# Attention with top-k, two MoE layers on one core: another order for epsilon, reciprocals, loads and the parts of a pair

## Chip, core and metric

The kernel runs on one core of one Trainium2 chip. The metric is the device time of one launch in microseconds (us); lower is better. Five engines take part, each with its own queue worked off in order: TensorE (PE), VectorE (DVE), ScalarE (ACT), GpSimd (POOL) and SyncE (SP), which here only issues DMAs.

## What is computed

Three layers follow one another on 4 batches of 576 tokens. Cut to what matters:

```python
scores = scale * np.matmul(q, k.transpose(0, 1, 3, 2))      # 4 batches, 8 heads, 576 x 64
kth = np.partition(scores, -32, axis=-1)[..., -32:-31]      # keep the 32 largest of a row
scores = np.where(scores >= kth, scores, -1e9)
attn = softmax(scores)
x = np.matmul(attn, v)                                      # -> 2304 x 512

h = x @ w_in                                                # MoE 1: 512 -> 2048 -> 512
x = (np.maximum(h, 0) + alpha * np.minimum(h, 0)) @ w_out

do = x @ w_skip > 0                                         # MoE 2: 8 experts, the best one per token
e = argmax(x[do] @ w_gate); p = its softmax weight
x[do] += p * (np.maximum(x[do] @ w1[e], 0) @ w2[e])
```

## The kernel before

Every product of 32-bit numbers is made of three matmuls on a rounded "high" part and the rest, the "low" part. ScalarE rounds the high part, and GpSimd makes the low part by a subtraction (helper `sub`, L109). So each operand of a matmul costs ScalarE one or two copies and GpSimd one subtraction.

Attention goes through 20 pairs of heads (4 pairs in each of 5 pieces of work: batch 0 in two pieces of 2 and 3 units, batches 1 to 3 in one piece of 5 units). A unit is 128 query rows of both heads; the last unit of a batch is a mixed one with the 64 left-over rows of both heads. There are 80 units, and one pass of the main loop (a step) works on several of them at once, at different stages. A step has 14 slots. The table `STEP` lists in which slot (first number) of the step of unit kx which stage is written, and for which unit (second number, relative to kx). After each slot the function `slot` adds deferred work (the list `late`, counted in slots) and a share of the MoE work (`todo`, `rowq`). The order so written is the order in each engine's queue; nothing is reordered later.

The stages of a unit: `scores` (PE, L390), `copy` (ACT takes the scores out of PSUM into sb, L395), `fold` (DVE, L411, six maxima and minima that sort the 576 scores roughly), four `round`s (DVE: MAX8 L420 finds eight maxima, MATCH_REPLACE8 L423 takes them out), `exp` (ACT, L443), `weights` (DVE, L449: masks the exponentials by the 32nd value and sums them), `eps` (ACT, L454: adds 1e-9 to the sum), `recip` (DVE, L458, and on ACT, L461, a copy of the reciprocals spread over 128 columns, tile rb), `turn` (PE transposes of the weights, L476 to L482), `evac` (ACT copies of them to PT, L488 to L499), `values` (PE, L506 and L510) and `out` (DVE multiplies by the reciprocal, L517; ACT and POOL make the two parts of x).

The parts of a pair (`heads`) prepare q and k for the next pair: `load` (six DMAs by SP into the tiles nat and nat_t, L315 and L316), `turn(0)` for q, `turn(1)` for k and `turn_t` for the 64 left-over rows. Each turn is a few PE transposes (L330, L336) into a PSUM tile pt, and `HL` = 3 slots later two ACT copies (L323, L324; for the left-over rows also L341, L344), followed by the POOL subtraction on 512 columns. The tile pt has two buffers, which the transposes of the weights use as well.

Two more things stand in the way of these stages. Before batch 0 is through, the 32 pieces of MoE 1's weights are converted (tile cv: ACT, DVE L278 and L279, POOL, and DMAs both ways). After each piece of work `rows` writes the routing for MoE 2: `logits` (PE L693, ACT copies lg, L700 and L702), `route` (DVE, from L737), and the ranks.

GpSimd's subtractions of MoE 1 (tile g) are held back by `between` in slots 9 to 13 and 0, until the fold is written; those of a pair's parts are not.

Of the kernel before, what the change touches and what calls it, by code (L numbers as in the profile page):

```python
# [8 lines left out]
F32R = mybir.dt.float32r  # L9
# [12 lines left out]
SPREAD = 1.0  # L22
NSLOT = 14
STEP = [(0, 2, "scores", 0), (0, 0, "exp", 0), (0, 0, "exp", 1), (0, 1, "fold"),
        (1, 2, "copy", 0), (1, -1, "eps"),
        (2, 1, "round", 0),
        (4, 2, "scores", 1), (4, -1, "turn", 0), (4, 1, "round", 1), (4, 2, "copy", 1),
        (5, -1, "recip"), (5, -1, "turn", 1),
        (6, -1, "evac", 0), (6, -2, "out"), (6, 1, "round", 2),
        (7, -1, "evac", 1),  # L30
        (8, 1, "round", 3), (8, 1, "rest"),
        (9, -1, "turn", 2),
        (10, 0, "heads"), (10, 0, "weights", 0), (10, -1, "evac", 2),
        (11, 0, "weights", 1),
        (13, -1, "values")]
AHEAD = 2
EC = 32
PH = 9
ECC = 1.9
CL = 2  # L40
DV = 8
# [18 lines left out]
def kernel(  # L60
# [241 lines left out]
    def heads(b, p, i):  # L302

        hd = dict(vb=vbd[i], qb=qbd[i])
        nats = {}

        def load():

            hd["q"] = att.tile([128, 2, SB], F32R, name="qT", tag="qT", bufs=2)
            hd["k"] = att.tile([128, 2, S + TL], F32R, name="kT", tag="kT", bufs=2)  # L310
            tail = att.tile([128, 2, D], F32, name="nat_t", tag="nat_t", bufs=2)
            for s, src in enumerate((q, k)):
                nat = att.tile([128, SF, 2, D], F32, name="nat", tag="nat", bufs=2)
                for h in range(2):
                    nc.sync.dma_start(nat[:, :, h, :], src[b, 2 * p + h, 0:SB, :].rearrange("(p r) d -> p r d", p=128))  # L315
                nc.sync.dma_start(tail[s * TL:(s + 1) * TL], src[b, 2 * p:2 * p + 2, SB:S, :].rearrange("h t d -> t h d"))  # L316
                nats[s] = nat
            nats[2] = tail

        def part(t, pt):  # L320

            raw = att.tile([128, 512], F32, name="raw_", tag="raw_", bufs=2)[:, 0:pt.shape[1]]
            nc.scalar.activation(t[:, 0], pt, AF.Copy)  # L323
            nc.scalar.activation(raw, pt, AF.Copy)  # L324
            sub(t[:, 1], raw, t[:, 0].bitcast(F32))

        def turn(s):
            pt = ptile()
            for r in range(SF):
                nc.tensor.transpose(pt[:, r * 128:(r + 1) * 128], nats[s][:, r].rearrange("p h d -> p (h d)"), ident)  # L330
            c0 = TL
            late.append((HL, lambda: part(hd["k"][:, :, c0:c0 + SB] if s else hd["q"], pt)))

        def turn_t():
            pt = ptile()
            nc.tensor.transpose(pt[:, 0:128], nats[2].rearrange("p h d -> p (h d)"), ident)  # L336

            def copies():

                raw = att.tile([128, 512], F32, name="raw_", tag="raw_", bufs=2)[:, 0:TL]  # L340
                nc.scalar.activation(raw, pt[:, 0:TL], AF.Copy)  # L341
                for h in range(2):
                    gp = slice(h * 64, (h + 1) * 64)
                    nc.scalar.activation(hd["qb"][gp, 0, gp], pt[gp, 0:TL], AF.Copy)  # L344
                    sub(hd["qb"][gp, 1, gp], raw[gp], hd["qb"][gp, 0, gp].bitcast(F32))
                part(hd["k"][:, :, 0:TL], pt[:, TL:128])
                nc.gpsimd.tensor_copy(hd["k"][:, :, S:S + TL], hd["k"][:, :, 0:TL].bitcast(F32))

            late.append((HL, copies))

        def loadv():
            vt = att.tile([128, 2, SF, D], F32, name="vt", tag="vt", bufs=2)
            hd["vt"] = vt
            nc.sync.dma_start(vt.rearrange("p h r d -> p h (r d)"),
                              v[b, 2 * p:2 * p + 2, 0:SB, :].rearrange("h (p r) d -> p h (r d)", p=128))
            for h in range(2):
                nc.sync.dma_start(vbd[i][h * 64:(h + 1) * 64, h * 64:(h + 1) * 64], v[b, 2 * p + h, SB:S, :])

        hd["v"] = loadv
        return hd, [load, lambda: turn(0), lambda: turn(1), turn_t]  # L360

    class Unit:

# [92 lines left out]
        def recip(self):  # L456
            st = self.st
            nc.vector.reciprocal(st[:, 2, self.n_], st[:, 1, self.n_])  # L458
            if not self.mix:
                self.rb = att.tile([128, 2, 64], F32, name="rb", tag="rb", bufs=2)  # L460
                nc.scalar.activation(self.rb, st[:, 2, :, None].to_broadcast([128, 2, 64]), AF.Copy)  # L461
# [218 lines left out]
    def rows(b, us, colof, x2t, hook, then):  # L680
# [121 lines left out]

            return [scatter] + none + [then]

        parts = [(lambda: not early[0] and rroom(), None), (0.1, logits), (0, None), (0.1, route)]
        for i in range(nu):
            parts += [(rroom, None), (0.45, lambda i=i: row(i)), (0, None)]
            if i == min(1, nu - 1):
# [266 lines left out]
    def main(work, exact, hooks=(lambda: [], lambda: [])):  # L1075
# [27 lines left out]
        last = {s_[0]: kx for kx, s_ in enumerate(steps)}  # L1103
        hds, hq, vq = {}, [], {}

        def push_heads(i):
            hd, parts = heads(*pairs[i], i % 2)
            hds[i] = hd
            hq.extend(parts)
            if i > 1:  # L1110

                vq[i] = hd["v"]
# [72 lines left out]
        for kx in range(-2, K + 2):  # L1185
# [19 lines left out]
            for x in range(NSLOT):  # L1205
# [3 lines left out]
                for at, d, name, *a in STEP:  # L1209
                    if at != x:  # L1210
                        continue
                    if name == "heads":
                        for f in hmine:
                            f()
                    elif d in U:
                        getattr(U[d], name)(*a)
# [204 lines left out]
```

## Time and profile before

| what | value |
|---|---|
| median of 3 runs | 1148.2 us (1145.6 to 1149.4) |
| profiled execution | 1146.64 us, its span 1144.8 us |
| busy: PE, DVE, ACT, POOL | 85%, 84%, 65%, 40% of the span |
| attention (first fold to last) | about 26 to 833 us |
| mean granted TensorE clock | 0.928 of full speed |

Busy shares are means over stages. From about 60 us to the end of attention DVE is busy nearly all the time; after it, the rest of MoE 1 and MoE 2 are carried by PE, then DVE and PE. PE's busy time is modelled, one matmul from its issue to its end, so that matmuls that follow closely count as overlapping; how close they can follow is read from trains of them.

### The profile page before, as it was taken

Reading aid. Unit: us, or ns where it says so; the run is one execution under the profiler, and the core shown is the slowest. Engines: PE = TensorE matmul, PEld = TensorE weight load, DVE = VectorE, ACT = ScalarE, POOL = GpSimd, SP = SyncE. Lnnn points to the kernel's source line nnn. Section 1 sums busy time; section 2 is a strip of 40 time slices with the busy share of each in tenths; the row PEclk is TensorE's granted clock in tenths of the full one; section 3 lists DMA queues with packets and bytes.
Section 4 is the critical chain, followed back from the end, with each engine's and each line's share of the span. In section 5 each row is a group of like instructions: output and inputs, shape, how many; then the busy total and the mean of one; then the engine's idle time right before and its main releaser. Section 6 shows DMA issues by size and latency. Waiting matters only on the chain.

```text
span 1144.8 us, 21810 instructions
## 1 busy us (share of the span) xinstructions
PE 976.2 (85%) x7214; PEld 855.7 (75%) x7214; DVE 957.6 (84%) x2906; ACT 738.7 (65%) x1970; POOL 453.9 (40%) x591
## 2 busy tenths in 40 slices
PE   1255657989898987898998999899999999898996
PEld 1143436879777875787997998789899999687884
DVE  5799999999999999999999889999933331799872
ACT  5576666866777665776677567767734452597761
POOL 5445543643334331244235344423435343228111
PEclk9996566999999995899999999999999999799998
DMA  8977764567544530224324253332337863699870
GB/s 233 336 220 229 216 184 124 188 191 232 187 136 154 179 130 21 69 75 142 97 84 142 75 171 93 105 122 75 112 111 274 298 221 111 195 372 385 316 276 15
DMA packets 129771, 197.37 MB, mean 172 GB/s; under 512 B 62766, under 2 KB 92462, under 8 KB 119408
## 3 DMA queue, kind: packets, MB, share of 16 engines
q1 hardware_dynamic: 115632, 107.48, 29.9%
q0 software_dynamic: 14016, 88.40, 22.6%
q8 instruction: 59, 0.97, 0.3%
q14 instruction: 64, 0.52, 0.2%
HBM read 167.44 MB, written 29.71 MB: 172 GB/s over the span
## 4 chain that ended last, share of the span: by engine, by line
PE 42%; DVE 42%; ACT 5%; issue 4%; DMA 4%; POOL 2%; SPq 1%; POOLq 0%; DVEq 0%; ACTq 0%
PE pm L627 14%; DVE v L420 8%; PE pm L578 8%; DVE F L411 6%; DVE Ex L449 6%; DVE F L423 5%; DVE m L411 5%; PE px L1003 4%; PE pm L985 3%; PE px L510 3%; PE pt L476 3%; PE ps L390 3%; DVE rn L595 3%; DMA nat<-in_q_dram 2%; DVE cv L278 2%
## 5 line engine op out<-in xcount | busy, mean ns | idle before, releaser
L627 PE MATMUL pm<-g,wr 128*128 128x288 f32 (+2 forms) x1536 | 237.3, 303 | 7.2 <-POOL g L109 7.2
L578 PE MATMUL pm<-x,wr 128*128 128x288 f32 (+2 forms) x1536 | 238.9, 304 | 4.0 <-ACT x L519 2.9
L627 PEld LDWEIGHTS pm<-g,wr 128*128 128x128 f32 x1536 | 209.0, 189 | 15.1 <-POOL g L109 8.8
L578 PEld LDWEIGHTS pm<-x,wr 128*128 128x128 f32 x1536 | 211.2, 191 | 10.4 <-issue 5.3
L420 DVE MAX8 v<-F 128x8 f32<-128x72 f32 (+2 forms) x576 | 214.0, 406 | 1.0
L395 ACT ACTIVATE sb<-ps 128x288 f32<-128x288 f32 x288 | 104.9, 411 | 89.3 <-PE ps L390 70.3
L109 POOL TENSOR_TENSOR g<-rn,g 128x288 fp32r<-128x288 f32 (+2 forms) x128 | 108.2, 853 | 123.2 <-ACT g L609 52.5
L390 PE MATMUL ps<-kT,qT 64*128 64x288 f32 x768 | 106.4, 363 | 38.6 <-ACT sb L395 15.7
L449 DVE SCALAR_TENSOR_TENSOR Ex<-sb,v,Ex 128x576 f32<-128x576 f32 x144 | 124.5, 891 | 0.0
L423 DVE MATCH_REPLACE8 F<-v,F 128x72 f32<-128x72 f32 (+1 forms) x432 | 122.7, 289 | 0.0
L390 PEld LDWEIGHTS ps<-kT,qT 64*128 64x128 f32 x768 | 69.2, 210 | 68.2 <-ACT sb L395 19.8
L109 POOL TENSOR_TENSOR x<-xf,x 128x128 fp32r<-128x128 f32 (+1 forms) x80 | 38.7, 483 | 177.6 <-ACT x L519 164.6
L443 ACT ACTIVATE Ex<-sb,st 128x576 f32<-128x576 f32 x144 | 105.0, 780 | 0.0
L595 DVE SCALAR_TENSOR_TENSOR rn<-rn,nalpha 128x288 f32<-128x288 f32 (+2 forms) x128 | 72.5, 566 | 34.3 <-ACT rn L589 31.7
L476 PE MATMUL pt<-ident,Ex 128*128 128x128 f32 x576 | 92.6, 302 | 0.0
L510 PE MATMUL px<-PT,vt 128*64 128x128 f32 (+1 forms) x1280 | 92.0, 292 | 0.0
L488 ACT ACTIVATE PT<-pt 128x512 f32<-128x512 f32 x144 | 86.0, 598 | 2.3 <-PE pt L476 2.0
L588 ACT ACTIVATE rn<-pm 128x288 f32<-128x288 f32 (+2 forms) x128 | 52.7, 412 | 45.3 <-PE pm L578 44.6
L476 PEld LDWEIGHTS pt<-ident,Ex 128*128 128x128 f32 x576 | 72.2, 154 | 11.1 <-issue 6.5
L510 PEld LDWEIGHTS px<-PT,vt 128*64 128x64 f32 x1280 | 72.5, 150 | 10.2 <-issue 2.9
L411 DVE TENSOR_TENSOR F<-m 128x144 f32<-128x144 f32 (+2 forms) x240 | 78.2, 377 | 0.0
L609 ACT ACTIVATE g<-rn 128x288 fp32r<-128x288 f32 (+2 forms) x128 | 56.4, 448 | 23.0 <-DVE rn L595 22.9
(367 smaller groups left out, 1839.2 us busy)
## 6 DMA issues: line engine op xcount, KB each, us to landing
wraw<-in_moe_w_dram SPq DMA_DIRECT2D x88, 512.0 KB, 6.0
wr<-win POOLq DMA_DIRECT2D x40, 1024.0 KB, 5.2
wr<-wout POOLq DMA_DIRECT2D x40, 1024.0 KB, 5.2
cv<-in_moe_w_in_dram SPq DMA_DIRECT2D x16, 512.0 KB, 5.3
win<-cv SPq DMA_DIRECT2D x16, 512.0 KB, 5.4
cv<-in_moe_w_out_dram SPq DMA_DIRECT2D x16, 512.0 KB, 4.1
wout<-cv SPq DMA_DIRECT2D x32, 256.0 KB, 4.5
vt<-in_v_dram SPq DMA_DIRECT2D x20, 256.0 KB, 3.0
```

The lines of the kernel that those rows point to most:

```text
L109: i = nc.gpsimd.tensor_tensor(o, a, b, op=OP.subtract)
L390: nc.tensor.matmul(self.ps[h, j][:, 0:HALF], lhsT=hd["q"][gp, a, u * 128:(u + 1) * 128], rhs=hd["k"][gp, b_, c0:c0 + HALF], **se)
L411: gate[0] = nc.vector.tensor_tensor(o[:, n_], a[:, n_, 0:w], a[:, n_, w:2 * w], op=op)
L420: nc.vector.max(v8[:, h, r, :], F[:, h, 0:w])
L423: nc.vector.match_replace(out=F[:, h, 0:w], in_to_replace=v8[:, h, r, :], in_values=F[:, h, 0:w], imm_value=NEG)
L443: nc.scalar.activation(self.Ex[:, h, :], self.sb[:, h, :], AF.Exp, bias=self.st[:, 0, h:h + 1], scale=0.125)
L449: nc.vector.scalar_tensor_tensor(Ex[:, h, :], sb[:, h, :], v8[:, h, 3, 7:8], Ex[:, h, :], op0=OP.is_ge, op1=OP.mult, accum_out=st[:, 1, h: ...
L476: nc.tensor.transpose(pt[:, c * 128:(c + 1) * 128], P[:, c0:c0 + 128], ident)
L510: nc.tensor.matmul(x[h * 64:(h + 1) * 64, 0:n], lhsT=hd["vt"][:, h, c, :], rhs=rhs, start=False, stop=(c == SF - 1))
L578: nc.tensor.matmul(hp[:, 0:n], lhsT=w[:, (f % 2) * 8 + a * 4 + d, :], rhs=x[:, d, c0:c1], start=(i == 0), stop=(i == 3 * KD - 1))
L595: nc.vector.scalar_tensor_tensor(rn[:, 0, 0:n], rn[:, 1, 0:n], nalpha[:, f:f + 1], rn[:, 0, 0:n], op0=OP.mult, op1=OP.add)
L627: nc.tensor.matmul(op_[:, 0:n], lhsT=w[:, 2 * f + a, :], rhs=g[(hf + ch) * 8 + f, sg][:, gg, 0:n], start=(i == 0), stop=(i == ni - 1))
```

## The change

The table of slots and four functions change.

- `eps` moves from slot 1 of the next step to slot 13 of the unit's own step, behind `weights`.
- `recip` keeps the DVE instruction and moves from slot 5 to slot 2, right behind the fold. The spread of the reciprocals becomes a stage of its own, `spread`, in slot 7 behind the second `evac`.
- The parts of a pair written in a step are dealt alternately to slot 3 and slot 10 (before: all in slot 10). In a step with one part, it goes to slot 3.
- The load of a pair's q and k goes to the end of the list of parts of the pair before it, so it is issued a pair ahead; the very first list has both loads. The tiles qT and kT are taken in `turn(0)` instead of in `load`.
- `route` is written `RD` = 5 slots after `logits` instead of one.

```diff
@@ STEP
         (0, 0, "exp", 0), (0, 0, "exp", 1), (0, 1, "fold"),
-        (1, 2, "copy", 0), (1, -1, "eps"),
-        (2, 1, "round", 0),
+        (1, 2, "copy", 0),
+        (2, -1, "recip"), (2, 1, "round", 0),
+        (3, 0, "heads", 0),
         (4, 2, "scores", 1), (4, -1, "turn", 0), (4, 1, "round", 1), (4, 2, "copy", 1),
-        (5, -1, "recip"), (5, -1, "turn", 1),
+        (5, -1, "turn", 1),
         (6, -1, "evac", 0), (6, -2, "out"), (6, 1, "round", 2),
-        (7, -1, "evac", 1),
+        (7, -1, "evac", 1), (7, -1, "spread"),
         (8, 1, "round", 3), (8, 1, "rest"),
         (9, -1, "turn", 2),
-        (10, 0, "heads"), (10, 0, "weights", 0), (10, -1, "evac", 2),
+        (10, 0, "heads", 1), (10, 0, "weights", 0), (10, -1, "evac", 2),
         (11, 0, "weights", 1),
-        (13, -1, "values")]
+        (13, -1, "values"), (13, 0, "eps")]
+RD = 5
...
@@ heads
-        return hd, [load, lambda: turn(0), lambda: turn(1), turn_t]
+        hd["load"] = load
+        return hd, [lambda: turn(0), lambda: turn(1), turn_t]
...
@@ Unit
         def recip(self):
             st = self.st
             nc.vector.reciprocal(st[:, 2, self.n_], st[:, 1, self.n_])
+
+        def spread(self):
+            st = self.st
             if not self.mix:
                 self.rb = att.tile([128, 2, 64], F32, name="rb", tag="rb", bufs=2)
                 nc.scalar.activation(self.rb, st[:, 2, :, None].to_broadcast([128, 2, 64]), AF.Copy)
...
@@ rows
-        parts = [(lambda: not early[0] and rroom(), None), (0.1, logits), (0, None), (0.1, route)]
+        parts = [(lambda: not early[0] and rroom(), None), (0.1, logits)] + [(0, None)] * RD + [(0.1, route)]
...
@@ main
         def push_heads(i):
-            hd, parts = heads(*pairs[i], i % 2)
+            if not ahead:
+                ahead[i] = heads(*pairs[i], i % 2)
+                hq.append(ahead[i][0]["load"])
+            hd, parts = ahead.pop(i)
             hds[i] = hd
             hq.extend(parts)
+            if i + 1 < len(pairs):
+
+                ahead[i + 1] = heads(*pairs[i + 1], (i + 1) % 2)
+                hq.append(ahead[i + 1][0]["load"])
...
                     if name == "heads":
-                        for f in hmine:
+                        for f in hmine[a[0]::2]:
                             f()
```

How the queues change shows best in the instructions themselves. Line numbers behind the change are those of the changed file (L454 eps is L458 there, L461 is L468, L323 and L324 are L322 and L323).

First ScalarE, one step in batch 1 in which k of the next pair is prepared (kT and raw are the two copies of the part, Ex the exponentials, sb the scores, st the sums, rb the spread reciprocals, PT the transposed weights, x the result). Before:

```order
L323 ACTIVATE kT<-pt 128x512
L324 ACTIVATE raw__4652<-pt 128x512
L443 ACTIVATE Ex<-sb,st 128x576 x2
L395 ACTIVATE sb<-ps 128x288 x2
L454 ACTIVATE st<-st 128x2
L636 ACTIVATE x2t<-pm 128x320
L395 ACTIVATE sb<-ps 128x288 x2
L461 ACTIVATE rb<-st 128x128
L488 ACTIVATE PT<-pt 128x512
L519 ACTIVATE x<-xf 128x64
L488 ACTIVATE PT<-pt 128x512
```

With the change:

```order
L458 ACTIVATE st<-st 128x2
L447 ACTIVATE Ex<-sb,st 128x576
L399 ACTIVATE sb<-ps 128x288 x4
L643 ACTIVATE x2t<-pm 128x320
L322 ACTIVATE kT<-pt 128x512
L323 ACTIVATE raw__4508<-pt 128x512
L495 ACTIVATE PT<-pt 128x512
L526 ACTIVATE x<-xf 128x128
L495 ACTIVATE PT<-pt 128x512
L468 ACTIVATE rb<-st 128x128
```

The epsilon now stands ahead of the exponentials and the score copies, the part's two copies behind them, and the spread behind both copies of PT.

Then VectorE, one step (xf is the result times its reciprocal, m and F are the fold's). Before:

```order
L449 SCALAR_TENSOR_TENSOR Ex,st<-sb,v_4423,Ex 128x576 x2
L411 TENSOR_TENSOR m<-sb 128x2x288
L411 TENSOR_TENSOR F<-sb 128x2x288
L411 TENSOR_TENSOR m<-m 128x2x144
L411 TENSOR_TENSOR F<-m 128x2x144
L411 TENSOR_TENSOR F<-m 128x2x72 x2
L420 MAX v_4423<-F 128x8 x2
L423 MATCH_REPLACE F<-v_4423,F 128x72 x2
L420 MAX v_4423<-F 128x8 x2
L423 MATCH_REPLACE F<-v_4423,F 128x72 x2
L458 RECIPROCAL st<-st 128x2
L517 TENSOR_TENSOR xf<-px,R 128x64
```

With the change:

```order
L453 SCALAR_TENSOR_TENSOR Ex,st<-sb,v_4447,Ex 128x576 x2
L415 TENSOR_TENSOR m<-sb 128x2x288
L415 TENSOR_TENSOR F<-sb 128x2x288
L415 TENSOR_TENSOR m<-m 128x2x144
L415 TENSOR_TENSOR F<-m 128x2x144
L415 TENSOR_TENSOR F<-m 128x2x72 x2
L462 RECIPROCAL st<-st 128x2
L424 MAX v_4447<-F 128x8 x2
L427 MATCH_REPLACE F<-v_4447,F 128x72 x2
```

The reciprocal stands two rounds earlier, with only the fold between it and the sums.

Last SyncE at the start of the program (cv and win are the weights to convert and converted, vt and vbd are v). Before, behind the loads of the first pair:

```order
L316 DMA nat_t<-in_k_dram 64x2x64
L254 DMA cv<-in_moe_w_in_dram 128x4x256 x3
L291 DMA win_127<-cv 128x1024
L254 DMA cv<-in_moe_w_in_dram 128x4x256
L354 DMA vt<-in_v_dram 128x2x256
L357 DMA vbd_93<-in_v_dram 64x64 x2
L291 DMA win_127<-cv 128x1024
```

and only nine rows further the loads of the second pair. With the change:

```order
L315 DMA nat_t<-in_k_dram 64x2x64
L256 DMA cv<-in_moe_w_in_dram 128x4x256 x2
L314 DMA nat<-in_q_dram 128x4x64 x2
L315 DMA nat_t<-in_q_dram 64x2x64
L314 DMA nat<-in_k_dram 128x4x64 x2
L315 DMA nat_t<-in_k_dram 64x2x64
L256 DMA cv<-in_moe_w_in_dram 128x4x256
```

The second pair's six loads follow two weight loads behind the first pair's.

## Rows read from the trace of the kernel before

**Rows 1.** Stretch; busy us of PE, PEld, DVE, ACT, POOL; clock, DMA share, GB/s.

```profile
60.00:180.00 120.00, 68.78 (x352) 49.78 (x351) 119.31 (x297) 84.43 (x211) 57.41 (x52) 0.68 0.67 202
500.00:700.00 200.00, 190.64 (x1622) 172.94 (x1620) 187.41 (x657) 138.29 (x423) 81.88 (x116) 0.98 0.37 115
700.00:850.00 150.00, 145.20 (x1246) 132.59 (x1243) 137.53 (x474) 102.72 (x315) 56.13 (x81) 1.00 0.30 100
```

**Rows 2.** Waits of DVE between 60 and 837 us: total, times, longest.

```profile
DVE st L458 <- ACT st L454: 13.6, 10, 2.8
DVE rc L737 <- ACT lg L702: 3.9, 1, 3.9
```

**Rows 3.** Timeline of DVE, 374 to 383 us: start, duration, line, operation.

```profile
374.75 1.83 DVE L411 TENSOR_TENSOR F<-sb 128x576 f32<-128x576 f32 x1
...
382.19 0.80 DVE L449 SCALAR_TENSOR_TENSOR Ex<-sb,v,Ex 128x576 f32<-128x576 f32 x1
...
382.92 1.90 DVE L449 SCALAR_TENSOR_TENSOR Ex<-sb,v,Ex 128x576 f32<-128x576 f32 x1
```

**Rows 4.** Timeline of POOL at the same times.

```profile
374.27 1.70 POOL L109 TENSOR_TENSOR qT<-raw__4521,qT 128x512 fp32r<-128x512 f32 x1 [2.35 <-ACT raw__4521 L324]
...
382.92 1.29 POOL L109 TENSOR_TENSOR kT<-raw__4652,kT 128x512 fp32r<-128x512 f32 x1 [2.00 <-ACT raw__4652 L324]
```

**Rows 5.** DVE's operations by line and shape, 60 to 850 us: total, mean ns.

```profile
L449 DVE SCALAR_TENSOR_TENSOR Ex<-sb,v,Ex 128x576 f32<-128x576 f32 x142 | 122.9, 892 | 0.0
...
L411 DVE TENSOR_TENSOR m<-sb 128x576 f32<-128x576 f32 x62 | 53.9, 870 | 0.0
L411 DVE TENSOR_TENSOR F<-sb 128x576 f32<-128x576 f32 x62 | 53.8, 868 | 0.0
```

**Rows 6.** One line's durations in ns, least, median and most.

```profile
L411 DVE TENSOR_TENSOR m<-sb x80: 442/748/1843, 26.1 to 831.3; 128x576 f32<-128x576 f32 x64, 128x288 f32<-128x288 f32 x16
```

**Rows 7.** A MAX8 pair on DVE under a subtraction on POOL, timeline.

```profile
81.41 1.27 POOL L109 TENSOR_TENSOR cv<-cv 128x512 fp32r<-128x512 f32 x1 [2.45 <-ACT cv L285]
...
82.19 0.81 DVE L420 MAX8 v<-F 128x8 f32<-128x288 f32 x2
...
370.45 0.81 DVE L420 MAX8 v<-F 128x8 f32<-128x288 f32 x2
```

**Rows 8.** The second pair's q at the start: PE, ACT, DVE, timeline.

```profile
34.81 1.09 PE L330 MATMUL pt<-ident,nat 128*128 128x128 f32 x4 [14.05 <-DMA nat<-in_q_dram]
...
35.93 0.60 ACT L323 ACTIVATE qT<-pt 128x512 fp32r<-128x512 f32 x1 [10.39 <-PE pt L330]
...
38.15 0.77 DVE L278 SCALAR_TENSOR_TENSOR cv<-cv 128x512 int32<-128x512 int32 x1 [7.08 <-ACT cv L274]
```

**Rows 9.** PE's operations between 500 and 700 us by line.

```profile
L627 PE MATMUL pm<-g,wr 128*128 128x288 f32 x384 | 62.1, 306 | 4.6 <-POOL g L109 4.6
L578 PE MATMUL pm<-x,wr 128*128 128x288 f32 x372 | 59.1, 304 | 0.0
```

**Rows 10.** The chain that ended last: a train of 192 matmuls, start and length.

```profile
920.21 25.44 PE pm L578 x192
```

**Rows 11.** PE's timeline in the step from 384.75 us.

```profile
386.25 1.09 PE L476 MATMUL pt<-ident,Ex 128*128 128x128 f32 x8
387.10 2.00 PE L627 MATMUL pm<-g,wr 128*128 128x320 f32 x12
389.65 0.33 PE L478 MATMUL pt<-ident,Ex 128*128 128x128 f32 x1 [0.55 <-ACT PT L488]
```

**Rows 12.** ACT's timeline around the same step.

```profile
381.75 0.60 ACT L323 ACTIVATE kT<-pt 128x512 fp32r<-128x512 f32 x1
...
382.72 1.44 ACT L443 ACTIVATE Ex<-sb,st 128x576 f32<-128x576 f32 x2
...
384.92 0.71 ACT L395 ACTIVATE sb<-ps 128x288 f32<-128x288 f32 x2 [0.76 <-DVE Ex L449]
```

**Rows 13.** ACT's wait for the reciprocal, whole run: total, times, longest.

```profile
ACT rb L461 <- DVE st L458: 43.2, 29, 3.6
```

More of the change, by code (lines that the diff above doesn't have):

```diff
@@ L307, in load @@
         def load():
-            hd["q"] = att.tile([128, 2, SB], F32R, name="qT", tag="qT", bufs=2)
-            hd["k"] = att.tile([128, 2, S + TL], F32R, name="kT", tag="kT", bufs=2)
             tail = att.tile([128, 2, D], F32, name="nat_t", tag="nat_t", bufs=2)
@@ L327, in turn @@
         def turn(s):
+            if s == 0:
+                hd["q"] = att.tile([128, 2, SB], F32R, name="qT", tag="qT", bufs=2)
+                hd["k"] = att.tile([128, 2, S + TL], F32R, name="kT", tag="kT", bufs=2)
             pt = ptile()
@@ L1104, in main @@
         hds, hq, vq = {}, [], {}
+        ahead = {}
         def push_heads(i):
-            hd, parts = heads(*pairs[i], i % 2)
+            if not ahead:
+                ahead[i] = heads(*pairs[i], i % 2)
+                hq.append(ahead[i][0]["load"])
+            hd, parts = ahead.pop(i)
             hds[i] = hd
             hq.extend(parts)
+            if i + 1 < len(pairs):
+                ahead[i + 1] = heads(*pairs[i + 1], (i + 1) % 2)
+                hq.append(ahead[i + 1][0]["load"])
             if i > 1:
```

## Prediction

> **What bounds the kernel now.** I read the stretches first: which engine has no idle time left, and where. From 60 to 180 us DVE is busy 119.3 of 120 us, from 500 to 700 us 187.4 of 200 [rows 1]. So through attention nearly every microsecond of DVE's own time, and every wait of DVE, is a microsecond of the kernel. Next I read DVE's waits there: 13.6 us in ten waits of the reciprocal for the epsilon, 3.9 us of the routing for the logits [rows 2]. That is little; the rest must be in the lengths of DVE's instructions. So the third view is one shape's mean against its undisturbed length. The masking (L449) takes 0.80 us when nothing disturbs it [rows 3] and 892 ns in the mean of 142; the two widest operations of the fold (L411) have a median of 748 ns [rows 6] and means of 870 and 868 ns [rows 5]. The timeline says why: the fold's second operation takes 1.83 us and a masking 1.90 us [rows 3] exactly where GpSimd makes the low part of q and of k for the next pair [rows 4]. Both operations read two tiles. MAX8 does not mind: a pair of them takes 0.81 us under a subtraction of GpSimd and 0.81 us without one [rows 7].
>
> The other engine near its limit is PE. Its busy time of 190.6 of 200 us [rows 1] is modelled and says little, so I count. In a train of 192 nothing but MoE matmuls, one takes 25.44 / 192 = 0.1325 us [rows 10]. From 500 to 700 us there are 384 + 372 of them [rows 9], 100 us; the other 1622 - 756 = 866 instructions take at most (387.10 - 386.25) / 8 = 0.106 us each, as eight transposes do [rows 11], 92 us. That is an upper bound of 192 of 200 us, 0.96. The value matmuls among the 866 are narrower, so I take 0.9. PE has little room there, more room elsewhere in attention.
>
> **The change part by part.** The sum is made against the profiled execution's own 1146.6 us (1144.8 of span and 1.8 around it); the median shown, 1148.2, lies 1.6 above it.
>
> *Parts of a pair in slot 3.* A part's copies stand three slots behind its transposes. Before, that was in front of the exponentials, so ScalarE reached them while DVE was at the masking, and GpSimd's subtraction fell on the masking and the fold. Now they stand behind the epsilon, the exponentials (1.44 us) and two pairs of score copies (0.71 us each) [rows 12]. Since the epsilon can't run before the masking ends, the subtraction starts at least 1.44 + 2 x 0.71 + 2 x 0.60 = 4.1 us after it, less overlaps of about 0.5 us. The fold is over by then; the rounds, which don't mind, are running. What the collisions cost: L449 (892 - 800) ns x 142 = 13.1 us, the two of the fold (870 - 748) x 62 = 7.6 and (868 - 748) x 62 = 7.4 us, together 28 us, a lower bound since the fold's narrower operations aren't in it. From the other side: 1.83 - 0.75 = 1.08 us for a q and 1.90 - 0.80 = 1.10 us for a k, 20 pairs, 44 us. I take 33 us. In the 8 pairs of batch 0, where a step has two parts, the k part stays in slot 10: 8 x 1.1 = 9 us stay. Gain 24 us (bounds: 0, if the subtractions meet other operations of DVE that read two tiles, and 44).
>
> [...]
>
> *Epsilon and reciprocal.* The epsilon no longer stands behind the exponentials, the first score copies, and with them PE's scores and a part that waits for nat. The reciprocal loses the cover of two rounds but keeps the fold. Of the 13.6 us I take 10 as gone; the rest stays where ScalarE arrives late from a copy that PE owes it. (Bounds: 0 and 13.6.)
>
> *The wait that is added.* ScalarE now stands at the epsilon until the second masking is done. Behind it are the next exponentials, needed 10 slots later, and the score copies, needed by the next fold. The exponentials start up to 2 x 0.8 = 1.6 us later per step. In exchange ScalarE no longer stands at the spread for DVE's reciprocal, 43.2 us in 29 waits [rows 13]; in slot 7 that is long done. ScalarE is busy 138 of 200 us [rows 1]; with 20 steps in it 20 x 1.6 = 32 us more make 170. So it fits, at no cost; if that cover were gone, each step would pay what is over.
>
> *Loads a pair ahead.* At the start PE waits 14.05 us for the second pair's q, ScalarE 10.39 us for PE, and DVE 7.08 us for ScalarE, with its conversions queued behind [rows 8]. SyncE now issues these six loads right behind two weight loads, ahead of all stores of converted pieces, instead of some 14 DMAs later. DVE's gap goes, but weight loads share the DMA queues: gain 6 of 7.1 us (bounds 0 and 7.1). Of later loads I count nothing: there DVE has no idle time that they could give back [rows 1, 2].
>
> *Routing five slots behind the logits.* The 3.9 us go, gain 3.5 us. The copies of the logits after attention are awaited too, but there PE sets the pace, so nothing is gained from those.
>
> Sum: 24 + 10 + 6 + 3.5 = 43.5 us, if PE follows. Some 20 of these fall between 500 and 850 us, where PE is 0.9 busy. As DVE gets faster there, PE's order of waits takes some of it back; I take off 40% of 20, 8 us. 1146.6 - 35.5 = 1111.
>
> **The rivals.** (B) *The subtractions collide again elsewhere*, with MoE's L595, with the conversions or, in mixed units, whose rounds are short, with the masking. For it: DVE's queue between the rounds holds such operations. Against it: the parts now start in the rounds by construction. Time: without the 24 us, and little for PE to take back, 6 + 10 + 3.5 - 2 = 17.5 us, 1129.
>
> (C) *Nothing that can be measured.* PE becomes the bound at once and the waits of DVE move from the reciprocal to the fold or to xf. For it: 0.96 as PE's upper bound. Against it: only 350 of the 800 us of attention are so full. Time 1143 to 1150.
>
> (D) *Slower: PE stands at the second transposition of the weights.* The tile pt has two buffers. The order in a step is now part, turn 0, turn 1, so turn 1 needs the buffer of the part, and the part's copies stand behind exponentials and score copies, some 3.9 us after the masking. PE is at turn 0 1.5 us after the fold's start and at the MoE matmuls behind it 0.85 us later [rows 11]. It would stand 3.9 - 1.5 - 0.4 = 2.0 us in place of 0.55 us at turn 2 [rows 11], 1.45 us more in each of the 36 steps of the 12 long pairs that have a part: 52 us, while 16 us of the gains above are left (batch 0 and the start). Against it: PE may run most of a step behind DVE, so that it arrives at turn 1 later and finds the buffer free. Only what exceeds PE's own slack counts, 0.1 x 10 us = 1.0 us per step: at 1.45 us it is 36 x 0.45 = 16 us, which the 16 us of gains just cover. So it is slower from 1.45 us upwards; with 0.35 us more, for transposes that start late by a MoE group, 36 x 0.8 = 29 us, 1146.6 - 16 + 29 = 1160.
>
> (E) *ScalarE as the bound by strict order.* [...] If ScalarE's 170 of 200 us were not enough because its work bunches between two waits, DVE would wait at the fold for the copies: 80 steps x 0.3 us = 24 us given back, 1135.
>
> **How the numbers follow.** My forecast, A: 0.58, 1098 to 1124. B: 0.16, 1125 to 1134. E: 0.06, 1130 to 1140. C: 0.08. D: 0.12, 1150 to 1183 (all 52 us). The predicted time is that of A, 1111. The range goes from 1094 (all 43.5 us and some of the narrower collisions) to 1140, which holds A, B and E. A change of under 0.3% (3.4 us) can't be told from none here. Faster: 0.58 + 0.16 + 0.06 = 0.80; within it: 0.08; slower: 0.12.
>
> **What would show it.** Right: the means of L449 and of the widest L411 fall to about 0.82 and 0.78 us, and GpSimd's 512-wide subtractions lie under MAX8 and MATCH_REPLACE8; the waits of the reciprocal fall below 4 us and the spread's wait vanishes; DVE's gap at 31 us is gone; attention ends some 35 us earlier and the time after it is unchanged. Wrong: new waits of DVE at the fold for sb or at xf for px; PE's turn 1 waiting for raw or kT for over 1 us a step; ScalarE's waits for the maskings growing past 1.6 us a step; the means of L449 and L411 as before with other partners.

## The result and the profile after

The change takes 1163.6 us (median of 4 runs, 1157.8 to 1164.7) where the kernel before takes 1146.9 beside it: ratio 1.0135 (95% interval 1.0108 to 1.0162). It is slower, by some 16 us; the forecast was 1111 us, so faster than before. The execution shown here took 1163.7 us, span 1161.9.

The same stretches as [rows 1], columns as there:

```profile
60.00:180.00 120.00, 72.40 (x377) 51.83 (x378) 118.97 (x318) 85.53 (x220) 57.07 (x59) 0.66 0.73 216
500.00:700.00 200.00, 182.59 (x1509) 163.69 (x1507) 176.49 (x613) 129.46 (x393) 74.20 (x108) 0.97 0.35 110
700.00:850.00 150.00, 141.03 (x1209) 126.94 (x1205) 145.63 (x488) 106.64 (x323) 60.14 (x79) 1.00 0.30 96
```

The first row does more than before: 377 instructions of PE in place of 352, 318 of DVE in place of 297. From 500 to 700 us it does less: PE 1509 in place of 1622, DVE 613 in place of 657, and both have more idle time, DVE 23.5 us in place of 12.6. So the early part gained and a later part lost. The start of each fold in DVE's timeline says how much and where. The 23rd fold, the third of batch 1, starts at 279.1 us (before: 291.4), so 12 us were gained up to there, 10.6 of them by the first fold of batch 1. The 80th and last starts at 845.8 (831.3). The 57 steps between took 566.7 us in place of 539.9: 27 us lost in batches 1 to 3. From the last fold to the end the change takes 2.5 us more.

DVE's operations by line and shape, 60 to 850 us, answering to [rows 5] (L449 is L453 now, L411 is L415):

```profile
L453 DVE SCALAR_TENSOR_TENSOR Ex<-sb,v,Ex 128x576 f32<-128x576 f32 x139 | 127.2, 943 | 0.0
...
L415 DVE TENSOR_TENSOR F<-sb 128x576 f32<-128x576 f32 x62 | 54.8, 885 | 0.0
L415 DVE TENSOR_TENSOR m<-sb 128x576 f32<-128x576 f32 x62 | 52.4, 844 | 1.4 <-ACT sb L399 1.2
```

The masking got longer, not shorter (943 ns, 892 before); the two of the fold stand at 885 and 844 (868 and 870). Forecast were 0.82 and 0.78 us. The place of the collisions did change: of the 14 subtractions for q from the tenth fold on, 9 meet a masking and 6 a fold, where before none met a masking and 12 a fold.

DVE's waits between 60 and 837 us, answering to [rows 2]:

```profile
DVE rc L744 <- ACT lg L709: 9.8, 2, 5.5
DVE rn L602 <- ACT rn L596: 8.7, 7, 2.8
DVE st L462 <- ACT st L458: 4.0, 3, 1.6
DVE tot L791 <- PE pm L780: 3.3, 2, 2.8
DVE rn L602 <- ACT st L432: 2.6, 2, 2.1
```

The reciprocal's wait fell from 13.6 to 4.0 us, about as forecast. In its place DVE waits for MoE's rn, and longer than before for the logits lg.

PE's transposes of the weights, from the page's list of groups (busy, mean ns | idle time ahead of them and what ended it):

```profile
L483 PE MATMUL pt<-ident,Ex 128*128 128x128 f32 x576 | 99.7, 305 | 44.4 <-ACT raw__584 L323 3.0 <-ACT raw__853 L323 2.5 <-ACT raw__1129 L323 2.0
```

This is rival (D)'s wrong sign: PE stands (is idle, waiting) 44.4 us at the turns for `raw`, the second copy of a part. One such step, in PE's timeline:

```profile
498.17 0.60 PE L333 MATMUL pt<-ident,nat 128*128 128x128 f32 x4
498.52 1.04 PE L585 MATMUL pm<-x,wr 128*128 128x288 f32 x6
499.49 0.66 PE L394 MATMUL ps<-kT,qT 64*128 64x288 f32 x6
500.08 0.66 PE L483 MATMUL pt<-ident,Ex 128*128 128x128 f32 x4
502.53 0.66 PE L483 MATMUL pt<-ident,Ex 128*128 128x128 f32 x4 [1.80 <-ACT raw__6290 L323]
502.95 1.83 PE L585 MATMUL pm<-x,wr 128*128 128x288 f32 x12
```

The part (498.17) and turn 0 (500.08) hold the two buffers of pt, so turn 1 stands until the part is copied out. ScalarE over the same time says why that is late:

```profile
494.88 0.20 ACT L458 ACTIVATE st<-st 128x2 f32<-128x2 f32 x1 [0.55 <-DVE Ex L453]
494.99 0.76 ACT L447 ACTIVATE Ex<-sb,st 128x576 f32<-128x576 f32 x1
496.82 0.41 ACT L595 ACTIVATE rn<-pm 128x288 f32<-128x288 f32 x1 [1.06 <-PE pm L585]
...
500.18 0.71 ACT L399 ACTIVATE sb<-ps 128x288 f32<-128x288 f32 x2 [1.72 <-PE ps L394]
500.78 0.42 ACT L595 ACTIVATE rn<-pm 128x288 f32<-128x288 f32 x1
501.07 0.43 ACT L596 ACTIVATE rn<-pm 128x288 f32<-128x288 f32 x1
501.36 0.63 ACT L322 ACTIVATE kT<-pt 128x512 fp32r<-128x512 f32 x1
501.84 0.64 ACT L323 ACTIVATE raw__6290<-pt 128x512 f32<-128x512 f32 x1
```

The epsilon runs at 494.88, right behind the masking. The part's first copy starts at 501.36 and its subtraction at 502.56, 7.7 us behind the epsilon, where the forecast had some 4 us: between them stand also MoE's evacuations (L595, L596, L616), and ScalarE waits 1.06 and 1.72 us for PE itself. Its stand at the epsilon itself is no longer than the forecast allowed. Up to 860 us it comes to (total, times, longest)

```profile
ACT st L458 <- DVE Ex L453: 50.0, 26, 3.7
```

against 1.6 us in each of 80 steps; it takes the place of the 43.2 us at the spread [rows 13], and single waits are up to 3.7 us. The subtraction on POOL (first row) and DVE (the other two) show what follows in this step:

```profile
502.56 1.31 POOL L111 TENSOR_TENSOR kT<-raw__6290,kT 128x512 fp32r<-128x512 f32 x1 [3.82 <-ACT raw__6290 L323]
```

```profile
502.64 1.84 DVE L453 SCALAR_TENSOR_TENSOR Ex<-sb,v,Ex 128x576 f32<-128x576 f32 x1
...
505.97 0.52 DVE L602 SCALAR_TENSOR_TENSOR rn<-rn,nalpha 128x288 f32<-128x288 f32 x1 [1.48 <-ACT rn L596]
```

The subtraction starts with the next masking, which takes 1.84 us in place of 0.80, and the MoE matmuls that stood behind turn 1 (502.95) make DVE wait 1.48 us for rn. So one step shows both: a collision that has stayed (k's masking took 1.90 us before [rows 3]) and a wait that is new.

### The profile page after: what moved, and what is told of

The parts are those of the page before. It is cut to its first block, busy times and chain, and to the rows that moved or that the text cites. A ratio compares the mean times of both kernels' runs of the same rounds, so it can differ in the third digit from the quotient of the medians.

```text
span 1161.9 us, 21789 instructions
## 1 busy us (share of the span) xinstructions
PE 984.3 (85%) x7214; PEld 856.1 (74%) x7214; DVE 962.4 (83%) x2906; ACT 742.1 (64%) x1970; POOL 455.9 (39%) x591
## 5 line engine op out<-in xcount | busy, mean ns | idle before, releaser
L585 PE MATMUL pm<-x,wr 128*128 128x288 f32 (+2 forms) x1536 | 243.4, 308 | 3.3 <-ACT rn L596 2.5
L585 PEld LDWEIGHTS pm<-x,wr 128*128 128x128 f32 x1536 | 215.9, 194 | 9.9 <-issue 5.1
L394 PE MATMUL ps<-kT,qT 64*128 64x288 f32 x768 | 103.2, 360 | 53.4 <-ACT sb L399 42.9
L483 PE MATMUL pt<-ident,Ex 128*128 128x128 f32 x576 | 99.7, 305 | 44.4 <-ACT raw__584 L323 3.0
L453 DVE SCALAR_TENSOR_TENSOR Ex<-sb,v,Ex 128x576 f32<-128x576 f32 x144 | 131.1, 938 | 0.0
L394 PEld LDWEIGHTS ps<-kT,qT 64*128 64x128 f32 x768 | 66.6, 208 | 81.8 <-ACT sb L399 46.3
L483 PEld LDWEIGHTS pt<-ident,Ex 128*128 128x128 f32 x576 | 70.2, 153 | 64.6 <-issue 5.9
L602 DVE SCALAR_TENSOR_TENSOR rn<-rn,nalpha 128x288 f32<-128x288 f32 (+2 forms) x128 | 75.9, 594 | 40.2 <-ACT rn L596 37.2
L595 ACT ACTIVATE rn<-pm 128x288 f32<-128x288 f32 (+2 forms) x128 | 52.8, 413 | 52.2 <-PE pm L585 44.5
L111 POOL TENSOR_TENSOR x<-xf,x 128x128 fp32r<-128x128 f32 (+1 forms) x80 | 50.3, 629 | 81.4 <-ACT x L526 79.6
L415 DVE TENSOR_TENSOR F<-m 128x144 f32<-128x144 f32 (+2 forms) x240 | 70.0, 343 | 0.0
L111 POOL TENSOR_TENSOR cv<-cv 128x512 fp32r<-128x512 f32 x32 | 45.1, 1408 | 55.8 <-ACT cv L287 39.7
```

The lines of the kernel that those rows point to most:

```text
L111: i = nc.gpsimd.tensor_tensor(o, a, b, op=OP.subtract)
L394: nc.tensor.matmul(self.ps[h, j][:, 0:HALF], lhsT=hd["q"][gp, a, u * 128:(u + 1) * 128], rhs=hd["k"][gp, b_, c0:c0 + HALF], **se)
L453: nc.vector.scalar_tensor_tensor(Ex[:, h, :], sb[:, h, :], v8[:, h, 3, 7:8], Ex[:, h, :], op0=OP.is_ge, op1=OP.mult, accum_out=st[:, 1, h: ...
L483: nc.tensor.transpose(pt[:, c * 128:(c + 1) * 128], P[:, c0:c0 + 128], ident)
L585: nc.tensor.matmul(hp[:, 0:n], lhsT=w[:, (f % 2) * 8 + a * 4 + d, :], rhs=x[:, d, c0:c1], start=(i == 0), stop=(i == 3 * KD - 1))
```

## The experiments

One table first. *Lengthening* is what DVE's instructions took above the lower quartile of their own shape and tiles, summed where over 60 ns; *between* is from the start of the 23rd to that of the 80th fold, and the three columns behind it hold for it, in us. The kernel before was run beside each set of kernels (medians 1146.9 to 1150.0 us), so ratios are compared, not times across sets. The columns behind the ratio come from one execution each, and executions of one kernel lie up to 14 us apart (e14), so a difference of 2 or 3 us between two rows says little.

| kernel | ratio to before, interval | 23rd fold | between | PE idle in it | DVE lengthening | DVE idle |
|---|---|---|---|---|---|---|
| before | 1 | 291.4 | 539.9 | 42.4 | 33.9 | 15.8 |
| change | 1.0135 (1.0108–1.0162) | 279.1 | 566.7 | 55.7 | 39.8 | 34.1 |
| e1 | 0.9960 (0.9943–0.9977) | 274.0 | 554.2 | 45.2 | 38.0 | 24.1 |
| e2 | 0.9984 (0.9965–1.0003) | 282.7 | 546.9 | 41.2 | 32.3 | 22.5 |
| e3 | 1.0112 (1.0077–1.0146) | 278.4 | 561.6 | 56.4 | 36.9 | 32.3 |
| e4 | 1.0104 (1.0058–1.0150) | 283.5 | 560.1 | 51.9 | 39.7 | 28.8 |
| e5 | 0.9963 (0.9934–0.9993) | 287.9 | 540.4 | 36.4 | 34.2 | 16.2 |
| e6 | 0.9741 (0.9680–0.9801) | 274.0 | 532.0 | 30.5 | 15.6 | 25.0 |
| e7 | 0.9883 (0.9833–0.9933) | 266.7 | 552.6 | 43.1 | 21.4 | 37.3 |
| e8 | 0.9891 (0.9833–0.9949) | 274.9 | 545.9 | 39.3 | 36.6 | 17.9 |
| e9 | 1.0091 (1.0067–1.0116) | 289.5 | 558.8 | 56.4 | 38.1 | 29.6 |
| e10 | 0.9937 (0.9908–0.9965) | 282.3 | 547.3 | 44.3 | 33.6 | 22.7 |
| e11 | 0.9967 (0.9945–0.9988) | 290.1 | 542.5 | 43.2 | 35.2 | 17.2 |
| e12 | 0.9817 (0.9771–0.9863) | 273.6 | 542.8 | 40.0 | 37.5 | 15.0 |
| e13 | 0.9863 (0.9839–0.9888) | 275.7 | 543.9 | 38.5 | 33.4 | 20.3 |
| e14 | 0.9918 (0.9887–0.9949) | 283.1 | 539.9 | 30.3 | 32.8 | 16.7 |

The first four runs asked which part of the change loses. Theory 1: PE's stand at turn 1. Theory 2: ScalarE's stand at the epsilon. Theory 3: routing five slots later.

**e1, e2: the stand, taken away in two ways.** In e1 the parts' transposes use the scores' three PSUM buffers; in e2 all parts are back in slot 10.

```diff
# e1, in turn(s) and turn_t
-            pt = ptile()
+            pt = psS.tile([128, 512], F32, name="ps", tag="ps")
# e2
-        (3, 0, "heads", 0),
-        (10, 0, "heads", 1), (10, 0, "weights", 0),
+        (10, 0, "heads", 0), (10, 0, "heads", 1), (10, 0, "weights", 0),
```

> The change, with the transposes of a pair's parts written into the scores' three PSUM buffers (ps) instead of the two that the transposes of the weights use (pt). Theory 1 (PE stands at the second transposition of the weights until ScalarE has copied the part out of pt: 25 us of PE's idle time in batches 1 to 3): that wait goes, and most of the loss with it, 1145 to 1152 us. Theory 2 (ScalarE stands at the epsilon and comes late with MoE's copies): 1160 to 1165, as with the change. Theory 3 (routing five slots later costs): 1160 to 1165.

> The change, with all parts of a pair back in slot 10; loads a pair ahead, epsilon, reciprocal, spread and routing as changed. Theory 1: PE's wait for the part goes, the collisions of q's and k's subtractions with masking and fold return; the gain of the early steps stays: 1135 to 1148 us. Theory 2: 1158 to 1165. Theory 3: 1158 to 1165.

Both undo the loss: 1144.1 and 1145.6 us, 20 and 18 under the change (e1 a little more than theory 1 had). In e1 the row of L483 reads

```profile
L483 PE MATMUL pt<-ident,Ex 128*128 128x128 f32 x576 | 93.2, 303 | 0.0
```

No idle time is left at the turns for `raw`. Theory 1 holds.

**e3, e4: epsilon and routing back.**

```diff
# e3
-        (1, 2, "copy", 0),
-        (2, -1, "recip"), (2, 1, "round", 0),
+        (1, 2, "copy", 0), (1, -1, "eps"),
+        (2, 1, "round", 0),
-        (5, -1, "turn", 1),
+        (5, -1, "recip"), (5, -1, "turn", 1),
-        (13, -1, "values"), (13, 0, "eps")]
+        (13, -1, "values")]
# e4
-RD = 5
+RD = 1
```

> The change, with the epsilon back in slot 1 of the next step and the reciprocal back in slot 5 (the spread stays in slot 7). Theory 1: the waits of the reciprocal return, some 10 us, PE's wait for the part stays: 1165 to 1175 us. Theory 2: ScalarE's copies come in time again: 1145 to 1155. Theory 3: 1163 to 1170.

> The change, with the routing one slot behind the logits again instead of five. Theory 1 and theory 2: within 4 us of the change, 1160 to 1168 us. Theory 3: the waits of the routing and of the ranks in batches 0 and 1 shrink, 1148 to 1156 us.

1159.8 and 1160.0 us: each is at most 4 us from the change, and the intervals overlap with it. Theories 2 and 3 explain no more than that each. e3 lies in none of its three ranges: theory 1 had it slower than the change, and the return of the reciprocal's waits cost nothing that can be told.

**e9, e10, e11: the split alone, with and without its own buffers.** e9 is the kernel before with loads a pair ahead and the parts dealt to slots 3 and 10; e10 adds e1's edit; e11 is the control, e1's edit with the loads and all parts in slot 10.

```diff
# e9 to e11: the change's push_heads and heads (loads ahead); e9, e10 also
         (2, 1, "round", 0),
+        (3, 0, "heads", 0),
-        (10, 0, "heads"), (10, 0, "weights", 0),
+        (10, 0, "heads", 1), (10, 0, "weights", 0),
-                        for f in hmine:
+                        for f in hmine[a[0]::2]:
```

> The kernel before with two edits of the change: loads a pair ahead (1146 us alone, in e5) and every other part of a pair in slot 3. Epsilon, reciprocal, spread and routing stay. Theory (the part in slot 3 alone makes PE stand at the first or second turn, because the part, turn 0 and turn 1 share two buffers): at least 8 us slower than e5, 1154 to 1166 us, and PE waits for raw at turn 1 for over 15 us in the whole run. Rival (the stand needs the late epsilon as well, which delays ScalarE): within 4 us of e5, under 1150 us.

> As e9, with the parts' transposes in the scores' PSUM buffers. Loads and split without the stand, and without the later epsilon, spread and routing. Theory (the rest of the loss in the steps 22 to 79, 14 us in e1, comes from the epsilon, the spread and the routing): these steps take 540 to 546 us and the time is 1128 to 1138 us, at least 6 us under e1. Rival (the rest comes from the split itself, whose subtractions meet x and g): 1141 to 1147 us.

> The kernel before with loads a pair ahead and the parts' transposes in the scores' PSUM buffers, all parts in slot 10. A control: if the scores' buffers by themselves help (PE no longer holds a buffer of the weights' transposes for a part), it is under 1141 us; if they matter only where the part stands ahead of the turns, it is within 4 us of e5's 1146 us.

e9 is slower than before (1161.6 us, as its theory had it), e10 faster (1144.6), e11 like e5, the loads alone (1147.5). So slot 3 with two shared buffers loses by itself, the late epsilon isn't needed for it, and the scores' buffers do nothing where no part stands ahead of the turns. The row of e9's turns over the whole run, with 78 us of idle time:

```profile
L478 PE MATMUL pt<-ident,Ex 128*128 128x128 f32 x576 | 98.1, 303 | 78.1 <-ACT raw__1408 L322 6.1 <-ACT raw__1131 L322 6.1 <-ACT raw__855 L322 5.2
```

e10 missed its theory: at 1144.6 us it lies in the rival's range, which put the rest of the loss on the split itself.

**e5: the loads alone.** The change's `push_heads` and `heads` in the kernel before, all parts in slot 10.

> The kernel before with one edit of the change alone: the loads of q and k are issued a pair ahead; all parts stay in slot 10, epsilon, reciprocal, spread and routing stay where they were. Theory 1 (the early gain of 7 us by step 10 and 12 us by step 22 comes from the loads at the start): 6 to 12 us faster than before, 1137 to 1142 us, the step starts of batch 0 ahead of before by that much and the lead kept to the end. Rival (the early gain comes from the parts and the epsilon, which stand elsewhere here): within 3 us of before. The prediction had 6 us for this edit.

1146.1 us, 0.37% (0.07 to 0.66) faster, 3.5 us earlier at the 23rd fold and nothing after it: the size lies between theory and rival. The gain is not at the start. DVE's gap there is 5.0 us in the change where [rows 8] had 7.08, but the first fold starts 3.0 us later than before (1.1 us in e5), and e5 is level with before as late as the eleventh fold. What e5 takes away is DVE's idle time from 60 us to the 23rd fold, 7.7 to 1.8 us, with it 4.5 us of waits for the epsilon.

**e6, e7: what the collisions of the parts cost.** Both leave out the low parts of q and k (zeros in their place), so they compute less than the others.

```diff
-            sub(t[:, 1], raw, t[:, 0].bitcast(F32))
+            nc.gpsimd.memset(t[:, 1].bitcast(F32), 0.0)
```

> The kernel before, with the computation changed: GpSimd fills the low parts of q and k (512 and 64 columns) with zeros in place of subtracting, so those instructions read no SBUF. It prices the collisions of the parts alone. Theory 1 (the prediction's price was right, the change only moved the collisions to other operations): the means of the masking and of the widest fold operations fall from 892 and 870 ns to about 0.82 and 0.78 us, and the time falls by 24 to 44 us, to 1103 to 1123 us. Rival (the collisions are mostly not on the path, because PE takes the time back): the means fall as much, the time by less than 15 us, above 1132 us. If the means stay, zeros written by GpSimd collide as well and the run says nothing on the price.

> The changed kernel with the parts' transposes in the scores' PSUM buffers (as in the run e1, 1144 us) and, the computation changed, zeros in place of the low parts of q and k. What the collisions of the parts still cost in the changed order. Theory 1 (the collisions cost as much in the new order as in the old, they only met other operations): the time falls below e1 by as much as the same edit takes from the kernel before. Rival (the new order has fewer collisions, and the gain of it is eaten by new waits of DVE and PE): the edit takes less than half of what it takes from the kernel before, under 12 us.

e6 takes 2.6% off, 28 us in 1122.3 against 1149.9 us, as its theory had it, though the means fell less than it said, to 860 ns for the masking and 789 and 770 ns for the two of the fold (60 to 820 us). A fill is also some 0.75 us shorter than a subtraction (0.53 us in the row below, 1.29 in [rows 4]), and what that gives is in the 28 us. A masking under such a fill keeps its 0.80 us (POOL, then DVE):

```profile
439.56 0.53 POOL L325 MEMSET qT<- 128x512 f32 x1
```

```profile
439.63 0.80 DVE L449 SCALAR_TENSOR_TENSOR Ex<-sb,v,Ex 128x576 f32<-128x576 f32 x1
```

The same edit on e1 (e7) takes only 0.8%, 9 us (1135.6 us): the rival of e7. The table shows why. Between the 23rd and 80th fold, e6 removes 18 us of lengthening and gains 8; e7 removes 17 and gains 2. DVE's idle time takes the rest, 9 and 13 us. In that stretch DVE does not set the pace alone.

**e8, e12: spread and routing.** e8 is e1 with the spread ahead of turn 1; e12 is e8 with `RD = 1`.

```diff
-        (5, -1, "turn", 1),
+        (5, -1, "spread"), (5, -1, "turn", 1),
-        (7, -1, "evac", 1), (7, -1, "spread"),
+        (7, -1, "evac", 1),
```

> The changed kernel with the parts' transposes in the scores' PSUM buffers (as e1, 1144 us) and the spread of the reciprocals in slot 5, ahead of the first turn, in place of slot 7 behind the evacuation. Theory: PE's 15 us of waits at turn 2 for rb between 280 and 840 us go, and since PE sets the pace there some of it comes off the time: 1132 to 1141 us. Rival: the wait only changes its name (PE waits at turn 1 for PT or ScalarE stands for the reciprocal instead): 1143 to 1147 us.

> As e8 (the change, parts in the scores' PSUM buffers, spread in slot 5; 1135.5 us) with the routing one slot behind the logits in place of five. Theory (the five slots bring nothing, since DVE waited 9.8 us for lg in the change against 3.9 before): 0 to 4 us faster than e8, 1131 to 1136 us. Rival (they do bring the 3.5 us that the prediction gave them): 1137 to 1141 us.

e8 took 1135.5 us, in its theory's range. PE's waits between 280 and 840 us in e1 name what went:

```profile
PE pt L486 <- ACT rb L468: 15.1, 24, 1.8
PE pt L485 <- ACT PT L495: 8.3, 16, 1.1
```

In e8 the first is gone and the stretch between the folds is 8 us shorter, so the spread in slot 7 cost 8 us once PE's larger stand was away. e12 took 1131.2 us, ratio 0.9817: 4 us under e8 by the medians, as theory had it, with intervals that overlap. e12 is the fastest kernel of this study that computes the whole, faster than before and than the change. It differs from e10 in the place of epsilon and reciprocal alone, and is 13 us faster: that is what the epsilon's edit is worth where PE doesn't stand. The forecast's mechanism is only part of it. Between the folds DVE's waits for the epsilon fall from 9.6 us to nothing and the stretch is 4.5 us shorter. The other 8.7 us are gained ahead of the 23rd fold, where from 60 us on e10 has no such wait and DVE's idle time is as in e12 (2.0 and 2.3 us); there the lengthening falls from 37.1 to 30.6 us, mostly under the conversions' subtractions. Why it does stays open.

**e13, e14: why the lengthening stayed, and what the split is worth.**

```diff
# e13, to e12, in push_heads
             hd, parts = ahead.pop(i)
+            if i and sum(1 for s_ in steps if s_[1] == i - 1) == 5:
+                parts = [lambda: None] + parts
# e14: e2's edit with e12's spread and RD, parts in pt
```

> As e12 (1131.2 us) with the parts of a five-unit pair one step later each. In e12 the part of q stands in the step whose rounds belong to the mixed unit; these rounds are half as long, and the subtraction, 4 to 5 us behind the start of the fold, meets the masking. One step later the rounds of a full unit run at that time. Theory (the collisions stayed because the clear stretch is too short in that step): q's subtractions in the steps from 10 to 79 meet the masking in under 4 of 14 places in place of 11 or more, and the lengthening of DVE's operations by q falls by 4 to 8 us. The time falls by less, 1 to 5 us, to 1126 to 1130 us, since PE sets the pace there. Rival (the place doesn't matter, ScalarE's lateness does): q meets the masking or the fold as often as before, and the time stays within 2 us of e12.

> The changed kernel with three parts taken back: all parts of a pair in slot 10, spread in slot 5, routing one slot behind the logits. What is left of the change is the loads a pair ahead and the epsilon behind the masking. Theory (the split is worth nothing: what it takes from the collisions PE's waits and the new meetings give back): 1128 to 1134 us, within 3 us of e12. Rival (the split in buffers of its own is worth the 9 us by which it shortens batch 0): 1136 to 1142 us.

e13 took 1132.8 us and missed: q's subtraction now starts mostly 5.6 to 8 us behind the fold's start and still meets the masking, in 9 of 14 places (e12: 11 of 14). The lengthening by q between the folds falls by 2.5 us only (9.4 to 6.9, counted as below). The short rounds of the mixed unit aren't the cause by themselves; ScalarE simply comes later in a full step. e14 missed its theory as well, that the split is worth nothing: it took 1137.1 us, in its rival's range, 1.0% behind e12 by the ratios (intervals 0.9771–0.9863 and 0.9887–0.9949), 7 us by the last fold. So the split in buffers of its own is worth 6 to 12 us, all of it ahead of the 23rd fold (which starts 9.5 us earlier; the stretch behind it is 2.9 us longer). Without the epsilon's edit it is less: e10 is 3 us ahead of e11 by the ratios, with intervals that overlap. Where the lengthening goes shows in the means, 60 to 820 us. e14, without the split:

```profile
L452 DVE SCALAR_TENSOR_TENSOR Ex<-sb,v,Ex 128x576 f32<-128x576 f32 x139 | 121.6, 902 | 0.0
...
L414 DVE TENSOR_TENSOR F<-sb 128x576 f32<-128x576 f32 x62 | 57.2, 922 | 0.0
...
L414 DVE TENSOR_TENSOR m<-m 128x288 f32<-128x288 f32 x62 | 40.0, 645 | 0.0
L601 DVE SCALAR_TENSOR_TENSOR rn<-rn,nalpha 128x288 f32<-128x288 f32 x64 | 35.5, 555 | 2.1 <-ACT rn L595 1.8 <-ACT st L431 0.3
```

and e12, with it:

```profile
L453 DVE SCALAR_TENSOR_TENSOR Ex<-sb,v,Ex 128x576 f32<-128x576 f32 x139 | 130.0, 962 | 0.0
...
L415 DVE TENSOR_TENSOR F<-sb 128x576 f32<-128x576 f32 x62 | 51.0, 822 | 0.0
...
L602 DVE SCALAR_TENSOR_TENSOR rn<-rn,nalpha 128x288 f32<-128x288 f32 x64 | 39.5, 617 | 4.4 <-ACT rn L596 2.2 <-ACT st L432 1.9 <-POOL x L111 0.3
...
L415 DVE TENSOR_TENSOR m<-m 128x288 f32<-128x288 f32 x62 | 34.9, 562 | 0.0
```

Two operations of the fold get shorter (922 to 822 and 645 to 562 ns), the masking (902 to 962) and MoE's rn (555 to 617) longer. Put the lengthening between the folds down to the subtraction that ended last before the lengthened operation did (the last section says why). Then q and k cost 19.2 us without the split and still 17.0 with it, and x and g rise from 9.3 to 16.6 us; from before to the change it is 21.3 to 18.6 and 8.8 to 18.1. So between the folds the parts' own collisions mostly changed their partner, and those of x and g came on top; ahead of the 23rd fold q and k do fall, from 17.6 to 12.6 us (e14 to e12). That the parts' subtractions, ahead of them in GpSimd's queue, push them there was not tried by itself.

## Why the prediction was wrong, step by step

**The failed step is rival (D), and the slack in it.** The mechanism was written down: pt's two buffers, part, turn 0, turn 1, and "Only what exceeds PE's own slack counts, 0.1 x 10 us = 1.0 us per step". The excess of 1.45 us a step was then held against a threshold of 1.45, and the rival got a chance of 0.12; the sum itself put the stand at nothing. The stand measured 1.24 us in the mean of 20 steps between the 23rd and the 80th fold (24.8 us), up to 1.8, and 19.6 us in 15 steps ahead of them, which the rival had left out. So its size was not underrated, and the rival counted more steps (36). The slack was smaller: with 1.0 us of it a step, 20 steps of 1.24 us would have cost 5 us, but e1, which takes away the stand and with it 10 us of PE's idle time, shortens the stretch between the folds by 12.5 us. The loss is larger where PE has less idle time. From the 23rd to the 50th fold, where PE was 0.87 busy before, the change loses 9 us and e1 gives back 5; from the 50th to the 80th, where it was 0.96, they are 18 and 7 us, with as long a stand (14 and 13 us, two at the mixed units' turn among them). The forecast's 0.9 took PE's rest as free time; but DVE and PE wait for one another, and DVE waits behind the matmuls that a standing PE holds back, as at 505.97. One thing stays open: PE's idle time between the folds rose by 13 us only, since most of its waits at turn 2 for PT went (13.0 to 0.8 us), and the stretch grew by 27. The rest is booked as busy time of PE, which is modelled.

**"So it fits, at no cost" was wrong for ScalarE's added wait.** ScalarE's share of busy time does allow it (129.5 of 200 us from 500 to 700). But its order put MoE's evacuations, two pairs of score copies and two waits for PE ahead of the part's copies, so the subtraction came 7.7 us behind the masking in place of 4, and PE stood for the copies. The stand at the epsilon was within the price (50.0 us in 26 waits); what was queued behind it, and waits for PE there, was not in it. The spread in slot 7, taken as free, cost 8 us (e1 to e8). Rival (E)'s 0.3 us a step at the fold is shown by no run: in the change the fold waits 1.2 us in all for ScalarE's copies (sb, 60 to 850 us).

**Parts in slot 3: the price was right, the place wrong.** 33 us of DVE's time for the collisions, bounds 28 and 44: e6 takes the lengthening over the whole run from 75.1 to 40.5 us, and 28 us off the time. The gain of 24 us didn't come, since the lengthening stayed (77.8 us in the change): rival (B) in kind, for which mixed units and L595 were named and which had 0.16. A masking took 0.80 us under a fill in e6 and 1.84 under a subtraction in the change. That the rounds don't mind held: from 60 to 850 us MATCH_REPLACE8 on 288 columns took 440 ns in the mean before and 439 in the change, MAX8 on 576 columns 746 and 745.

**PE's share given back, 8 us, was too small.** It was 40% of 20 us, for 500 to 850 us. By e6, 56% of what DVE gains between the 23rd and the 80th fold is given back in the old order (18.3 us removed, 8.0 gained), by e7 90% in the new one.

**Epsilon and reciprocal: right for the wait, the size in part luck.** 10 us forecast; DVE's wait fell by 9.6, and the edit is worth 13 us where it can show (e10 to e12). But 8.7 of these come ahead of the 23rd fold, where there was no wait left to remove.

**Loads ahead: near the size, by another way.** 6 us forecast, 4 measured (e5). The gap at the start, from which the 6 us were worked out, gave nothing; the gain came from DVE's waits between 60 us and the 23rd fold, of which the prediction counted nothing.

**Routing: no gain seen.** A gain of 3.5 us was forecast; DVE's wait for lg rose from 3.9 to 9.8 us, and one slot in place of five is 4 us faster in both pairs of kernels (change to e4, e8 to e12). That points to the wrong sign, but each time within what the intervals leave open. Why the wait grows stays open: in e12 too it is 7.1 us.

Added up from the ratios: loads -4, split in shared buffers +15 (e5 to e9), spread +8, routing +4 and epsilon -13 make +10, against +16 measured. The epsilon gives nearly nothing while PE stands (e3), so the terms don't simply add.

## What to carry to other kernels

When a producer is written ahead of others that take from the same few buffers, follow the oldest buffer to the instruction that frees it, along that engine's queue with its own waits, before asking whether the wait fits into anyone's idle time. In this kernel, where two engines are both over 0.9 busy (PE 0.95 and DVE 0.94 from 500 to 700 us before), a stand found little slack to hide in, and more than half of what one engine saved was given back (56% by e6). Moving the colliding subtractions left DVE's lengthening where it was, 75.1 us before and 77.8 in the change: between the folds that of q and k fell from 21.3 to 18.6 us, and that of x and g rose from 8.8 to 18.1. So look where a colliding instruction lands in its new place, and where those queued behind it land.

## What the runs showed of the hardware

In e6 a fill by GpSimd of 128 x 512 took 0.53 us, and the masking that it overlaps took 0.80 us (439.63); in the change a subtraction of the same size took 1.31 us, and the masking that it overlaps 1.84 us (502.64). Whether the subtraction's reading, its writing or its length makes the difference, these two runs don't show.

How long a masking or a fold's operation took went with the end of the subtraction. In the rows of one step above, the subtraction ends at 503.87 us and the masking at 504.48; in [rows 3] and [rows 4] the two pairs end at 384.21 and 384.82, and at 375.97 and 376.58: 0.61 us each time. In the two traces, before and change, all 83 maskings and widest operations of the fold that took at least 0.15 us above their undisturbed 0.80 and 0.75 us end 0.61 to 0.63 us after a GpSimd subtraction does. From this comes the estimate used above: most of such an operation's own time lies behind the subtraction's end (0.61 of 0.80 us), so the lengthening is put down to the subtraction that ended last before it, not to one that merely began under it.
